# When a weight conversion's stages run beside attention: two orders of the same instructions

## The chip, the cores and the metric

The kernel runs on one core of a Trainium2 chip. The metric is the device time of one execution in microseconds (us); less is better. The engines named below: TensorE (PE; PEld is its loading of stationary operands), VectorE (DVE), ScalarE (ACT), GpSimd (POOL) and SyncE (SP, which here only issues DMAs). Each engine works through its own list of instructions in order; semaphores tie the lists together.

## The reference

An RWKV-6 attention is followed by a two-layer projection with a gated activation. All of it is float32 or wider.

```python
for t in range(S):                                   # B=4, H=8, S=768, D=48
    cur = np.einsum('bhd,bhe->bhde', u[None] * kt, vt)
    y[:, :, t] = np.einsum('bhd,bhde->bhe', rt, state + cur)
    state = wt[:, :, :, None] * state + np.einsum('bhd,bhe->bhde', kt, vt)
...
x = y.transpose(0, 2, 1, 3).reshape(B * S, H * D)    # 3072 tokens of 384
h = x @ w_in                                         # 384 x 2048
sp = np.maximum(h, 0.0) + np.log1p(np.exp(-np.abs(h)))
g = h * erf(sp)
out = g @ w_out                                      # 2048 x 384
```

The two weights come as 64-bit floats (the arrays are divided by a 64-bit square root), and the kernel itself turns them into float32.

## The kernel before

**Steps.** The work goes in 12 steps, counted from 0 here. A step is 128 tokens of a pair of batches. `attend(s, ...)` does the attention of steps 0 to 4, `attend_late` that of the later ones. The attention of a step runs over six levels: at level n, 32 pairs of small matmuls on TensorE (L444, in `level_products`) write products of k and r to a PSUM buffer, VectorE scales r and k by products of decays (L260, in `scale`), and VectorE copies the products under a mask into the tile `own` (L456; at level 1 it is a multiplication, L661; at level 6 ScalarE copies, L463). Level n+1 works on the scaled r and k. After level 6, `from_own` multiplies `own` by v on TensorE (L478), k is transposed (L673) and copied to `kT` by ScalarE (L677), `state_part` makes the state's increments (L530), and VectorE and GpSimd bring the state up to date (L703 or L701, L704, L706). `through_state` adds the old state's part (L504), and ScalarE copies y to `xT` (L511 to L514), part of it by six small DMAs (L518).

**PSUM buffers.** `products` hands out one of two buffers, `pp0` and `pp1`. While weights are being converted it always gives `pp0`, because the conversion uses `pp1`. Two further buffers, `m`, hold the results of the projections.

**The projections beside it.** Pieces of the feed-forward part are put between the levels, so that TensorE has work while VectorE and ScalarE finish a level: `hidden` makes two F tiles of h (L742, 12 matmul records a piece, then a copy to SBUF by ScalarE, L751), `project` multiplies the gated h by w_out (L771, result copied at L780). Softplus and erf (L724, L727, ScalarE) and the gating product (L731, VectorE) are taken from a list by `advance`. Steps 1 and 2 have only `hidden` pieces of the step before.

**The conversion.** The weights are turned from 64-bit to 32-bit floats in 16 pieces, 8 of w_in and 8 of w_out, in `convert`, a generator to which single letters are sent. One piece takes: a load by SyncE (`l`, L196) into one of three buffers `words`; a pair of ScalarE operations (`s`: L209 to `pp1` from the high words, L211 to `rest` from the low words); a shift in place by VectorE (`h`, L217, in `pp1`); an OR of the sign by VectorE (`o`, L225, which reads `words` and `pp1` and writes the weight); and an integer add of `rest` by GpSimd (L229). `j` stands for `ho`. The next `s` needs the `o` before it, for `pp1`; the load three pieces later needs that `o` too.

**The order.** Nothing is scheduled by a planner: the order in which the Python code issues instructions is the order on each engine. `place(n)` is called at the end of level n+1 (0 to 5), and then at 6 after the transposes and 7 after the state; it sends the letters of `CONVERT[s][n]`, then issues a projection piece. The letters for place 8 are sent by `behind()` at the step's end. In step 1 at level 2, `behind(None)` sends the letters of `BEHIND_SCALING` between the scaling and the masked copy. In step 1, `products(..., 1)` puts the state part into `pp1`.

```python
CONVERT = (
    ("", "", "", "", "", "s", "jls", "j", "sl"),
    ("hl", "jsl", "jsl", "jsl", "jl", "sj", "", "", "sl"),
    ("jsl", "jsl", "jsl", "jsl", "jl", "sj", "s"),
    ("js", "j"),
)
BEHIND_SCALING = "os"
```

## Time and profile before

| what | us |
|---|---|
| median of 3 runs (616.69, 619.03, 617.15) | 617.15 |
| the profiled execution | 616.69 |
| its span, first to last instruction | 614.9 |
| TensorE busy in the span | 602.1 |
| VectorE, ScalarE, GpSimd busy | 409.3, 293.9, 293.3 |
| L742 (first projection), TensorE busy, and L771 (second) | 257.3 and 252.1 |
| one piece of `hidden` on TensorE (L742 x12) | 2.86 |
| step 1 between the starts of its first and last L742 | 34.55 to 66.37 |
| step 2 likewise | 68.93 to 96.75 |

The profile page gives shares of the span by engine. The timeline that is quoted further down has one row for each instruction or run of equal ones: start in us from the span's start, length in us, engine, line, operation, output and inputs, and in square brackets the idle time of the engine before it, with what ended it. [...] "SPq" and "ACTq" rows are DMAs being issued. Matmul ends are modelled.

### The profile page before, as it was taken

The page shows a single profiled execution, that of the slowest core. Times are in us where ns is not written, and L with a number is a line of the kernel's source. Part 1 is how long each engine was busy: PE and PEld are TensorE (multiplying, and loading weights), DVE is VectorE, ACT ScalarE, POOL GpSimd, SP SyncE. Part 2 cuts the span into 40 slices and gives each one's busy share as a digit, 9 for nine tenths or more (in the row PEclk, how much of TensorE's full clock was granted, in tenths as well). Part 3 has the DMA queues.
Part 4 walks back from the last instruction along what each step waited for, and adds up shares of the span by engine and source line. Part 5 has one row for each costly group of instructions (what it writes and reads, how often), then busy time and mean ns, then how long its engine had stood idle before and what let it go on. Part 6 is the DMA issues. An engine that isn't in the chain of part 4 may idle for free.

```text
span 614.9 us, 15592 instructions
## 1 busy us (share of the span) xinstructions
PE 602.1 (98%) x6858; PEld 445.9 (73%) x6858; DVE 409.3 (67%) x459; ACT 293.9 (48%) x374; POOL 293.3 (48%) x295
## 2 busy tenths in 40 slices
PE   7889999999999999999999999999999999999997
PEld 6668787678668668668668768768768768668654
DVE  5687696995995897897797797797797311110300
ACT  2548888544446724534534534534534444624600
POOL 4348184603497399299199299299296000000000
PEclk9999999999999999999999999999999999999999
DMA  8376471440353316307307306405303100000000
GB/s 325 117 281 203 184 258 58 164 149 8 136 157 78 101 34 190 112 29 206 101 30 197 109 31 181 126 31 156 117 28 79 25 26 0 9 26 1 0 27 26
DMA packets 51371, 63.27 MB, mean 103 GB/s; under 512 B 34920, under 2 KB 40296, under 8 KB 49896
## 3 DMA queue, kind: packets, MB, share of 16 engines
q1 hardware_dynamic: 50152, 61.68, 31.5%
q8 instruction: 54, 0.88, 0.6%
q10 hardware_dynamic: 1152, 0.59, 0.4%
q14 instruction: 13, 0.11, 0.1%
HBM read 52.39 MB, written 8.69 MB: 99 GB/s over the span
## 4 chain that ended last, share of the span: by engine, by line
PE 85%; DVE 6%; DMA 3%; POOL 2%; issue 2%; ACT 1%; SPq 0%; POOLq 0%; ACTq 0%; DVEq 0%
PE m L771 38%; PE m L742 37%; PE pp L444 4%; DMA w<-in_rkw 3%; PE y L478 2%; PE y L504 1%; PE pp L530 1%; DVE in L260 1%; POOL w_in_sb L229 1%; DVE w_in_sb L225 1%; POOL tot_sb L312 1%; PE pp L673 1%; DVE sums L364 1%; DVE pp L217 1%; DVE own L456 1%
## 5 line engine op out<-in xcount | busy, mean ns | idle before, releaser
L742 PE MATMUL m<-xT,w_in_sb 128*128 128x256 f32 x1152 | 257.3, 382 | 2.4 <-DVE w_in_sb L225 1.2
L771 PE MATMUL m<-w_out_sb,h 128*128 128x384 f32 x768 | 252.1, 488 | 0.0
L742 PEld LDWEIGHTS m<-xT,w_in_sb 128*128 128x128 f32 x1152 | 216.1, 190 | 34.8 <-issue 3.6
L771 PEld LDWEIGHTS m<-w_out_sb,h 128*128 128x128 f32 x768 | 144.6, 190 | 98.5
L751 ACT COPY h<-m 128x512 f32<-128x512 f32 x96 | 56.1, 584 | 130.5 <-PE m L742 130.4
L731 DVE TENSOR_TENSOR h<-h,sp 128x1024 f32<-128x1024 f32 x48 | 74.6, 1594 | 52.1 <-ACT sp L727 51.9
L260 DVE TENSOR_TENSOR in<-in,tot_sb 128x1024 f32<-128x1024 f32 (+1 forms) x60 | 84.4, 1414 | 30.6 <-PE pp L444 27.3
L378 POOL TENSOR_TENSOR words<-words,rest 128x528 f32<-128x528 f32 (+10 forms) x77 | 85.7, 1113 | 6.0
L374 POOL TENSOR_TENSOR rk<-words 128x528 f32<-128x528 f32 (+3 forms) x28 | 44.5, 1588 | 81.2 <-DVE sums L364 70.8
L780 ACT COPY o<-m 128x384 f32<-128x384 f32 x24 | 11.5, 480 | 110.3 <-PE m L771 110.3
L312 POOL TENSOR_TENSOR tot_sb<-tot_sb 128x256 f32<-128x256 f32 (+4 forms) x60 | 54.6, 911 | 4.5
L727 ACT ACTIVATE sp<-sp 128x2048 f32<-128x2048 f32 x24 | 45.9, 1911 | 0.3
L724 ACT ACTIVATE sp<-h 128x2048 f32<-128x2048 f32 x24 | 45.9, 1911 | 0.3
L444 PEld LDWEIGHTS pp<-in 48*64 48x64 f32 (+1 forms) x2368 | 33.8, 125 | 16.3 <-issue 8.5
L364 DVE TENSOR_REDUCE sums<-words 128x6 f32<-128x288 f32 (+8 forms) x66 | 29.2, 470 | 19.4 <-POOL words L374 19.2
L444 PE MATMUL pp<-in 48*64 48x64 f32 (+1 forms) x2368 | 38.3, 212 | 3.7 <-issue 1.6
L727 ACT ACT_TABLE_LOAD x24 | 30.8, 1283 | 15.9 <-issue 13.0
L374 POOL TENSOR_TENSOR words<-words 128x336 f32<-128x336 f32 (+6 forms) x49 | 35.1, 716 | 3.8
L364 DVE TENSOR_REDUCE sums<-rk 128x14 f32<-128x672 f32 (+9 forms) x54 | 34.8, 704 | 0.2
L724 ACT ACT_TABLE_LOAD x24 | 30.8, 1283 | 4.9 <-issue 4.5
L378 DVE TENSOR_TENSOR words<-words,rest 128x576 f32<-128x576 f32 (+8 forms) x34 | 27.9, 820 | 1.2
L229 POOL TENSOR_TENSOR w_out_sb<-w_out_sb,rest 128x768 int32<-128x768 int32 x8 | 17.8, 2222 | 17.8 <-DVE w_out_sb L225 17.7
(80 smaller groups left out, 438.0 us busy)
## 6 DMA issues: line engine op xcount, KB each, us to landing
in<-in_rkw SPq DMA_DIRECT2D x11, 1024.0 KB, 5.6
words<-in_moe_w_in SPq DMA_DIRECT2D x8, 768.0 KB, 4.5
words<-in_moe_w_out SPq DMA_DIRECT2D x8, 768.0 KB, 4.3
words<-in_rk_rows SPq DMA_DIRECT2D x8, 768.0 KB, 6.8
w<-in_rkw SPq DMA_DIRECT2D x11, 512.0 KB, 8.4
v<-in_v SPq DMA_DIRECT2D x12, 384.0 KB, 6.9
out<-o SPq DMA_DIRECT2D x24, 192.0 KB, 1.9
rest<-in_w_rows SPq DMA_DIRECT2D x8, 384.0 KB, 7.3
```

Of the source, the lines that this page charges most:

```text
L260: nc.vector.tensor_mul(halves, halves, view(tots[level - 1], 0, [[1, n], [2, nb], [0, half]]))
L312: nc.gpsimd.tensor_mul(new, pair[:, :, 0], pair[:, :, 1])
L364: nc.vector.tensor_reduce(out=view(sums[:], n, [[near * (NEAR + 1), NEAR // near], [NEAR + 1, near - n]]), in_=terms[n], axis=mybir.AxisLi ...
L374: engine.tensor_mul(terms[n], r[:, :, n:], k[:, :, : near - n])
L378: engine.tensor_mul(k[:, :, :m], k[:, :, :m], w[:, :, n : n + m])
L444: nc.tensor.matmul(pp[s0 : s0 + m, e, n, :m], lhsT=rk[rows(e), 1, n, s0 : s0 + m], rhs=rk[rows(e), 0, n, t0 : t0 + m], start=True, stop=True,)
L724: nc.scalar.activation(held[0][:], h[:], AF.Softplus)
L727: nc.scalar.activation(held[0][:], held[0][:], AF.Erf)
L731: nc.vector.tensor_mul(h[:, part], h[:, part], held[0][:, part])
L742: nc.tensor.matmul(ps[:, ff, :], lhsT=w_in_sb[:, g * FG + f + ff, kk * P : (kk + 1) * P], rhs=xT[:, kk, :], start=kk == 0, stop=kk == KT - 1,)
L751: nc.scalar.copy(h[:, f : f + FT, :], ps[:])
L771: nc.tensor.matmul(ps[j][:], lhsT=gs[g][:, f, j * C : (j + 1) * C], rhs=w_out_sb[:, g * FG + f, :], start=g + f == 0, stop=g == NG - 1 and ...
```

## The change

The stages of the conversion take other places in steps 1 and 2, and the state part of step 1 takes the other PSUM buffer. No instruction is added or taken away on any engine:

- VectorE: in step 1 at level 2, the OR (L225) comes before the scaling (L260), not after it.
- ScalarE: in step 1, one pair L209, L211 (piece 3) comes ahead of the first copy L751 of the step. In steps 1 and 2 at level 6, one pair (pieces 7 and 13) comes ahead of the second of two copies L751 and of the copies of `own` (L463), not after them. In step 2 the pair after that (piece 14) comes behind L463, ahead of the copies of h and `kT`, not after `kT`.
- TensorE: the order is the same; the state part of step 1 (L530) writes `pp0`, and so the first products of step 2 (L444) get a wait for VectorE (L706).
- GpSimd and SyncE: the same order.

```diff
--- before.py
+++ after.py
@@ -125,11 +125,9 @@
 
     turns = {"next": 0, "converting": False}
 
-    def products(shape, n=None):
-
-
-        if n is not None:
-            return ps_p.tile(shape, FP32, name=f"pp{n}")
+    def products(shape):
+
+
         n = 0 if turns["converting"] else turns["next"]
         turns["next"] = 1 - n
         return ps_p.tile(shape, FP32, name=f"pp{n}")
@@ -211,35 +209,29 @@
                 nc.scalar.mul(out=rest[:], in_=low.bitcast(U32), mul=2.0**-29)
                 held[i] += [base.bitcast(I32), rest]
 
-        def shift(i):
-            if i in held:
-                bits = held[i][1]
-                nc.vector.tensor_scalar(
-                    out=bits, in0=bits, scalar1=3, scalar2=None, op0=ALU.logical_shift_left
-                )
-
         def join(i):
             if i in held:
                 words, bits, rest = held.pop(i)
                 into = weights[i][0].bitcast(I32)
+                nc.vector.tensor_scalar(
+                    out=bits, in0=bits, scalar1=3, scalar2=None, op0=ALU.logical_shift_left
+                )
                 nc.vector.scalar_tensor_tensor(
                     out=into, in0=words[:, :, :, 1], scalar=-(1 << 31), in1=bits,
                     op0=ALU.bitwise_and, op1=ALU.bitwise_or,
                 )
                 nc.gpsimd.tensor_tensor(out=into, in0=into, in1=rest[:], op=ALU.add)
 
-        stages = {"l": load, "s": scale, "h": shift, "o": join}
-        done = dict.fromkeys(stages, 0)
+        done = {"l": 0, "s": 0, "j": 0}
         for _ in range(3):
             load(done["l"])
             done["l"] += 1
         while True:
             what = yield
-            for stage in {"j": "ho"}.get(what, what):
-                stages[stage](done[stage])
-                done[stage] += 1
+            {"l": load, "s": scale, "j": join}[what](done[what])
+            done[what] += 1
             if weights[0][1].dtype != FP32:
-                turns["converting"] = 0 < done["s"] and done["o"] < len(weights)
+                turns["converting"] = 0 < done["s"] and done["j"] < len(weights)
                 turns["next"] = 0
 
     def rows(e, n=D):
@@ -652,8 +644,6 @@
             keep_busy(DM, DM // 2)
             if level == 1 and s == 1:
                 stay_warm()
-            if s == 1 and level == 2:
-                behind(None)
             got = pp[:].rearrange("p e n t -> p (e n) t")
             if level == 1:
                 if not s:
@@ -687,8 +677,7 @@
 
 
         if s:
-
-            ps = products([P, NC, JP, HC], 1 if s == 1 else None)
+            ps = products([P, NC, JP, HC])
             ps = [ps[:, h] for h in range(NC)]
         else:
             ps = [ps_m.tile([P, JP, HC], FP32, name="m") for h in range(NC)]
@@ -827,12 +816,10 @@
 
     CONVERT = (
         ("", "", "", "", "", "s", "jls", "j", "sl"),
-        ("hl", "jsl", "jsl", "jsl", "jl", "sj", "", "", "sl"),
-        ("jsl", "jsl", "jsl", "jsl", "jl", "sj", "s"),
+        ("jsl", "jsl", "jsl", "jsl", "jsl", "j", "", "", "sl"),
+        ("jsl", "jsl", "jsl", "jsl", "jsl", "js"),
         ("js", "j"),
     )
-
-    BEHIND_SCALING = "os"
 
     STAGES = {
         1: (0, 0, 0, 0, 0, 0, 1, 0), 2: (1, 0, 0, 0, 0, 0, 1, 1), 3: (1, 2, 1, 0, 0, 2, 1, 1)
@@ -900,14 +887,7 @@
             if s > DIRECT:
                 attend_late(s, place)
                 continue
-            def behind(n=0):
-                if n is not None:
-                    convert_at(LOG + 2)
-                    return
-                for what in BEHIND_SCALING:
-                    conversion.send(what)
-
-            attend(s, xTs[s], place, behind)
+            attend(s, xTs[s], place, lambda: convert_at(LOG + 2))
             if s + 2 < n_steps:
                 load_step(s + 2)
                 if s + 2 == DIRECT:
```

## The prediction

> **What bounds the kernel now.** I read the page from the top: busy shares, then the chain that ended last, then the same chain in order of time, and last the timeline of steps 1 and 2 (counted from 0; the change's words call them steps two and three), where every moved instruction stands.

> From the page, busy times and the shares of the chain:

> ```profile
> PE 602.1 (98%) x6858; PEld 445.9 (73%) x6858; DVE 409.3 (67%) x459; ACT 293.9 (48%) x374; POOL 293.3 (48%) x295
> ...
> PE 85%; DVE 6%; DMA 3%; POOL 2%; issue 2%; ACT 1%; SPq 0%; POOLq 0%; ACTq 0%; DVEq 0%
> ```

> TensorE bounds nearly everything. So the change is worth what it adds to or takes from TensorE's waits between 35 and 105 us; no instruction is added or removed on any engine. Where TensorE has a wait, some other engine is the bound for a moment. The first one is at level 2 of step 1 (timeline: start, length, engine, line):

> ```profile
> 39.02 1.23 DVE L260 TENSOR_TENSOR in<-in,tot_sb 128x1024 f32<-128x1024 f32 x1 [1.41 <-PE pp L444]
> 40.16 0.95 DVE L225 SCALAR_TENSOR_TENSOR w_in_sb<-words,pp 128x768 int32<-128x768 int32 x1
> 41.03 1.34 DVE L456 COPY_PREDICATED own<-mask_sb,pp 128x512 f32<-128x512 int32 x1
> 41.14 0.88 ACT L209 ACTIVATE pp<-words 128x768 f32<-128x768 f32 x1 [2.66 <-DVE w_in_sb L225]
> 41.17 7.06 SPq L196 DMA_DIRECT2D words<-in_moe_w_in  x3
> 41.25 1.83 POOL L229 TENSOR_TENSOR w_in_sb<-w_in_sb,rest 128x768 int32<-128x768 int32 x1 [3.96 <-DVE w_in_sb L225]
> ...
> 42.52 1.16 PE L444 MATMUL pp<-in 48*64 48x64 f32 x64 [0.78 <-DVE own L456]
> ```

> VectorE idles 1.41 us for the level's products, then runs the scaling, the OR of a weight piece and the masked copy; TensorE waits 0.78 us for that copy. Two other places show what VectorE's scaling costs when a GpSimd add (L229) is already running:

> ```profile
> 71.80 1.83 POOL L229 TENSOR_TENSOR w_out_sb<-w_out_sb,rest 128x768 int32<-128x768 int32 x1 [6.71 <-DVE w_out_sb L225]
> ...
> 73.23 1.49 DVE L260 TENSOR_TENSOR in<-in,tot_sb 128x1024 f32<-128x1024 f32 x1 [1.57 <-PE pp L444]
> ...
> 117.56 2.41 POOL L229 TENSOR_TENSOR w_out_sb<-w_out_sb,rest 128x768 int32<-128x768 int32 x1
> 118.34 2.25 DVE L378 TENSOR_TENSOR words<-words,rest 128x576 f32<-128x576 f32 x1
> ```

> The scaling takes 1.49 instead of 1.22 us when it meets the last 0.40 us of the add, and ends 1.09 us after it. The second pair is the strong case: a product of 576 elements takes 2.25 us where its neighbour of 672 took 0.86, and it ends 0.62 us after the add.

> The ends of the two steps, level 6 and what follows:

> ```profile
> 54.26 0.59 ACT L751 COPY h<-m 128x512 f32<-128x512 f32 x1 [0.29 <-PE m L742]
> 54.27 0.95 DVE L225 SCALAR_TENSOR_TENSOR w_in_sb<-words,pp 128x768 int32<-128x768 int32 x1
> 54.95 1.18 ACT L463 COPY own<-pp 32x512 f32<-32x512 f32 x2
> 55.04 2.86 PE L742 MATMUL m<-xT,w_in_sb 128*128 128x256 f32 x12
> 56.04 0.86 ACT L209 ACTIVATE pp<-words 128x768 f32<-128x768 f32 x1
> 57.83 0.67 PE L478 MATMUL y<-own,v 64*48 64x64 f32 x32
> ...
> 65.13 1.12 DVE L706 TENSOR_TENSOR s<-faded,pp 48x384 f32<-48x384 f32 x2 [0.95 <-POOL faded L704]
> 65.33 1.11 PE L444 MATMUL pp<-rk 48*64 48x64 f32 x64
> ...
> 68.93 3.14 PE L742 MATMUL m<-xT,w_in_sb 128*128 128x256 f32 x12 [1.00 <-DMA xT<-y]
> ...
> 87.88 0.95 DVE L225 SCALAR_TENSOR_TENSOR w_out_sb<-words,pp 128x768 int32<-128x768 int32 x1
> 88.55 1.18 ACT L463 COPY own<-pp 32x512 f32<-32x512 f32 x2
> 89.64 0.86 ACT L209 ACTIVATE pp<-words 128x768 f32<-128x768 f32 x1
> 91.23 0.67 PE L478 MATMUL y<-own,v 64*48 64x64 f32 x32
> ```

> In both steps the copies of own (L463) end well before TensorE's L478 needs them, because ScalarE does its next conversion pair (L209, L211) after them. The chain in order of time shows that step 1 ends on ScalarE, not TensorE: from kT at 59.55 without a gap through the softplus, y, xT and its DMA to 68.93.

> **The change part by part.** Weight pieces are numbered from 0; #2 is the first one joined in step 1.

> *1. Level 2 of step 1: the OR moves ahead of the scaling.* VectorE's order becomes shift, OR, scaling, copy. The shift starts at 36.66 and an OR follows a shift by 1.0 us (26.52 to 27.53), so the OR runs 37.66 to 38.61, in what was idle. Taken alone this ends the scaling at 40.25 and the copy at 41.5, and TensorE's level 3 would start when L742 ends, 41.74: a gain of 0.78. But the OR releases GpSimd's add, which follows its end by 0.14 (41.11 to 41.25): 38.75 to 40.58. The scaling comes at 39.02, behind it. By the 71.80 row it ends 1.09 after the add, at 41.67, instead of 40.25. The copy starts 0.09 before that end (as at 40.16) and takes 1.34: 42.92. TensorE follows by 0.15: 43.06, against 42.52. **Loss 0.54.** [...]
> Bounds: -0.78 (no meeting) to +0.67 (its whole 1.22 run after the add); I take 0.54, by the nearest row. In before the scaling starts first and the add waits (2.68 us at 44.36); at levels 3 to 5 both queues move by the same 0.54, so that order stays.
> Moved with it: ScalarE's pair #3 goes ahead of the copy of h (37.90 to about 40.35); the buffer it frees is wanted by the L742 of 43.61, so the 3 us between hide it. The load that waits for the OR (SP, 41.17) goes out at 38.65; its piece is first used at 47.87+0.54, and the slowest later landing was 9.2 us, so it is in time. What it shares the queues with, step 2's inputs, is wanted from 49.97.

> *2. Level 6 of step 1: pair #7 goes ahead of the second copy of h and of L463.* L209 must wait for the OR of #6 to free its PSUM buffer. In the clock of before: OR ends 55.22, L209 at 55.26, L211 0.84 later, the copy of h 0.82 later (56.92), L463 0.49 later, 57.41 to 58.59. TensorE would start L478 at 57.90. Its first two matmuls need only the first half of own; the third starts at 58.65, and the remaining 14 of 16 take 0.52: 59.17 against 58.49. **Loss 0.68** (bounds: 0.1, if the first half's end at 58.0 were enough, to 1.0 with 0.15 of latency at each of two hand-overs). Behind L478 stand the transposes, kT and the whole ScalarE chain to 68.93: it moves by 0.54+0.68.

> *3. Step 1's state part in the first buffer.* L444 of the next step must now wait for L706, ending at 66.25: it starts at 66.35 instead of 65.33, 1.02 late. Behind it: its own 1.04 and six matmuls (66.37 to 67.93, 1.56), then the L742 that waits until 68.93 for xT. That wait of 1.00 takes it: 66.35+1.04+1.56 = 68.95. **Loss 0.0 to 0.1, 0.05 taken.** If xT came earlier, up to 1.0 would show.

> *4. Level 6 of step 2: pair #13 likewise.* OR ends 88.83; L209 88.87, L211 89.71, copy of h 90.53, L463 91.02 to 92.20. L478 starts its third matmul at 92.25 and ends 92.77, against 91.30+0.59 = 91.89. **Loss 0.88** (bounds 0.3 to 1.2, worked like part 2). Here TensorE has no other wait: every row from 72.07 to 145.77 in the chain is its own, so all of it counts. Pair #14 now precedes the copies of h and kT: kT ends at 95.05 instead of 93.75, and the state part that needs it starts at 95.44+0.88; hidden by one L742 group of 2.75.

> *Downstream.* At 146.77 VectorE starts on TensorE's L530 after an idle 5.80, and carries the chain to 171.74; it starts later by what TensorE is late. Nothing there is tied to a fixed time, so I subtract nothing.

> *Sum.* 0.54+0.68+0.05+0.88 = 2.15 us. The profiled execution took 616.69 (span 614.9 and 1.8 around it): 618.84. It is 0.46 below the median of 617.15, so against the median: 619.3.

> **The rivals.**
> *A, the add does not block the scaling.* Then part 1 gains 0.78, part 2 gives 0.68 back, part 3's tie holds step 1's end where it is, and only part 4 counts: 617.15+0.88 = 618.0. For it: at 9.38 the scaling beside short GpSimd products took only 1.53. Against: the 118.34 row.
> *B, not slower.* One place, 146 to 172: VectorE's chain there takes up the delay because ScalarE's and GpSimd's results, not TensorE's, set its pace; price -2.15, time 617.2. It decides if the work at 146.77 could start 2 us later and the level at 171.74 were still on time. For it: there is 1.42 and 0.80 of issue time inside this stretch of the chain. Against: the 5.80 wait at its head and the 0.33 that TensorE waits at its end.
> [...]
> A fall of the granted clock I count under C: the rows show 1.00 throughout, even in 32 to 36 us, where TensorE was busy 2.75 of 4; the new waits (1.3, 0.8, 1.0, 0.9) leave no longer gap. [...]

> **How the numbers follow.** Sum as worked out: 0.5. A: 0.17. B: 0.08. C: 0.25. The likeliest is 619.3. Their bounds give 617.9 (0.3 for part 1, 0.1, 0, 0.3) to 620.1 (0.67, 1.0, 0.1, 1.2); to hold 8 in 10 I reach to A below and C above: 617.6 to 620.9. The 0.5% that a measurement can tell from no change is 3.1 us: slower means over 620.24, most of C and a tail of the sum, since the three runs of before lie 2.3 apart: 0.27. Faster (under 614.06) has no case of its own: 0.02. The rest, 0.71, lies within.

> **What the profile after would show.** Part 1: the OR near 37.7, the add near 38.75, the scaling longer than 2 us, the level-3 L444 near 43.1. Part 2 and 4: L209 before L463, and L478 waiting 0.7 to 1.0 on ScalarE's own. Part 3: the rk L444 waiting about 1 us on L706 and the wait on xT gone or nearly. Wrong if the scaling keeps 1.23, if L478 does not wait, if the granted clock falls, or if the delay at 100 us differs from the delay at 175 us.

## The result, and the profile after

The changed kernel took 620.38 us (median of 4 runs, 620.20 to 620.52) where the kernel before took 617.30 on the same chip (4 runs, 616.69 to 619.03): a ratio of 1.0045 with a 95% interval of 1.0025 to 1.0066. That is 3.1 us or 0.5% more. The profiled execution took 620.44 us, with a span of 618.7; against the profiled execution before (616.69) it is 3.75 longer. 620.38 lies inside the range forecast, 1.1 above the value forecast. As will be seen, the sum of the four parts was priced well (2.15, measured 2.06), and 1.8 us of the 3.75 came from a place that was priced at nothing.

In the changed kernel the lines named here are numbered 2 to 11 lower: L444 has become L436, L260 L252, L225 L219, L229 L223, L456 L448, L209 L207, L463 L455, L478 L470, L706 L695, L742 L731, L504 L496, L771 L760.

The page of the changed kernel, busy times and the shares of the chain that ended last:

```profile
PE 602.6 (97%) x6858; PEld 446.0 (72%) x6858; DVE 411.5 (67%) x459; ACT 293.4 (47%) x374; POOL 292.8 (47%) x295
...
PE 86%; DVE 7%; issue 2%; ACT 2%; DMA 1%; POOL 1%; SPq 0%; DVEq 0%; ACTq 0%; POOLq 0%
```

TensorE works as long as before (602.6 against 602.1), so the added time is TensorE standing still. Level 2 of step 1, in the timeline of the changed kernel (start, length, engine, line, and in brackets the idle time and what ended it):

```profile
37.55 0.95 DVE L219 SCALAR_TENSOR_TENSOR w_in_sb<-words,pp 128x768 int32<-128x768 int32 x1
38.64 1.83 POOL L223 TENSOR_TENSOR w_in_sb<-w_in_sb,rest 128x768 int32<-128x768 int32 x1 [1.46 <-DVE w_in_sb L219]
38.92 2.64 DVE L252 TENSOR_TENSOR in<-in,tot_sb 128x1024 f32<-128x1024 f32 x1 [0.42 <-PE pp L436]
41.48 1.27 DVE L448 COPY_PREDICATED own<-mask_sb,pp 128x512 f32<-128x512 int32 x1
42.90 1.16 PE L436 MATMUL pp<-in 48*64 48x64 f32 x64 [1.26 <-DVE own L448]
```

GpSimd's add starts 0.28 ahead of VectorE's scaling, which then takes 2.64 in place of 1.23 and ends 1.09 after the add (41.56 against 40.47). TensorE waits 1.26 in place of 0.78. The ends of steps 1 and 2 and the start of step 2, in the same view:

```profile
55.65 0.88 ACT L207 ACTIVATE pp<-words 128x768 f32<-128x768 f32 x1 [1.29 <-DVE w_in_sb L219]
57.73 1.17 ACT L455 COPY own<-pp 32x512 f32<-32x512 f32 x2
58.95 0.65 PE L470 MATMUL y<-own,v 64*48 64x64 f32 x28 [0.28 <-ACT own L455]
...
66.25 1.11 DVE L695 TENSOR_TENSOR s<-faded,pp 48x384 f32<-48x384 f32 x2 [0.95 <-POOL faded L693]
67.51 1.16 PE L436 MATMUL pp<-rk 48*64 48x64 f32 x64 [0.88 <-DVE s L695]
68.60 1.78 PE L731 MATMUL m<-xT,w_in_sb 128*128 128x256 f32 x7
...
90.04 0.88 ACT L207 ACTIVATE pp<-words 128x768 f32<-128x768 f32 x1 [1.30 <-DVE w_out_sb L219]
92.11 1.17 ACT L455 COPY own<-pp 32x512 f32<-32x512 f32 x2
93.33 0.65 PE L470 MATMUL y<-own,v 64*48 64x64 f32 x28 [0.28 <-ACT own L455]
```

At both step ends ScalarE does the conversion pair first, the copies of own come late, and all but four of the matmul records that read own follow the second copy. At 67.51 TensorE waits 0.88 for VectorE, and the 1.00 that it waited before on xT is gone: L731 goes straight on at 68.60.

Following one marker after another through both traces (start in the changed kernel less start before, us):

| marker | delay |
|---|---|
| step 1's first shift (chance difference of the start) | -0.11 |
| level 3 of step 1 | +0.38 |
| transposes after level 6, step 1 | +1.12 |
| level 2 of step 2 | +1.17 |
| transposes after level 6, step 2 | +2.09 |
| first L771 (101.73 before) | +1.94 |
| the L771 after VectorE's stretch (172.74 before) | +1.95 |
| L504 run at 249.31 before | +1.97 |
| what follows that run | +2.17 |
| L504 run at 435.62 before | +2.19 |
| what follows that run | +3.75 |
| last run of L771 (570.21 before) | +3.75 |

The last jump is the surprise. It lies 330 us behind the last changed instruction, where both kernels issue the same instructions. The chain in order of time (start, length, what), first of the kernel before, then of the changed one:

```profile
435.62 1.19 PE y L504 x64
436.81 5.36 PE m L771 x16
```

```profile
437.81 0.33 PE y L496 x21
438.14 1.55 issue
439.69 0.87 PE y L496 x43
440.56 1.49 PE m L760 x4
```

In the middle of a run of 64 small matmul records, with nothing to wait for, TensorE issues nothing for 1.55 us ("issue" is time in which the engine waited for nothing that the profile shows). The same run takes 2.75 in place of 1.19. A gap of the same kind near 250 us exists in both kernels (0.94 before, 1.09 after); the run around it took 2.05 before and 2.24 after, which is the other +0.20.

### The profile page after: what moved, and what is told of

It reads as the page before. It is cut to its first block, busy times and chain, and to the rows that moved or that the text cites. A ratio compares the mean times of both kernels' runs of the same rounds, so it can differ in the third digit from the quotient of the medians.

```text
span 618.7 us, 15586 instructions
## 1 busy us (share of the span) xinstructions
PE 602.6 (97%) x6858; PEld 446.0 (72%) x6858; DVE 411.5 (67%) x459; ACT 293.4 (47%) x374; POOL 292.8 (47%) x295
## 4 chain that ended last, share of the span: by engine, by line
PE 86%; DVE 7%; issue 2%; ACT 2%; DMA 1%; POOL 1%; SPq 0%; DVEq 0%; ACTq 0%; POOLq 0%
PE m L760 38%; PE m L731 37%; PE pp L436 5%; DVE in L252 2%; PE y L470 2%; PE pp L522 1%; PE y L496 1%; DMA in<-in_rkw 1%; PE pp L663 1%; DVE pp L216 1%; DVE sums L356 1%; DVE words L370 1%; DVE own L448 1%; DVE w_in_sb L219 0%; ACT own L455 0%
## 5 line engine op out<-in xcount | busy, mean ns | idle before, releaser
L731 PE MATMUL m<-xT,w_in_sb 128*128 128x256 f32 x1152 | 257.2, 382 | 1.4 <-DVE w_in_sb L219 1.2
L760 PE MATMUL m<-w_out_sb,h 128*128 128x384 f32 x768 | 252.1, 488 | 0.0
L731 PEld LDWEIGHTS m<-xT,w_in_sb 128*128 128x128 f32 x1152 | 216.1, 190 | 33.7 <-issue 2.4
L760 PEld LDWEIGHTS m<-w_out_sb,h 128*128 128x128 f32 x768 | 144.6, 190 | 98.5
L252 DVE TENSOR_TENSOR in<-in,tot_sb 128x1024 f32<-128x1024 f32 (+1 forms) x60 | 85.9, 1440 | 29.9 <-PE pp L436 28.2
L304 POOL TENSOR_TENSOR tot_sb<-tot_sb 128x256 f32<-128x256 f32 (+4 forms) x60 | 52.8, 880 | 4.5
L436 PEld LDWEIGHTS pp<-in 48*64 48x64 f32 (+1 forms) x2368 | 33.8, 125 | 16.6 <-issue 10.5
L436 PE MATMUL pp<-in 48*64 48x64 f32 (+1 forms) x2368 | 38.4, 212 | 4.1 <-DVE own L448 1.4
L223 POOL TENSOR_TENSOR w_out_sb<-w_out_sb,rest 128x768 int32<-128x768 int32 x8 | 17.8, 2231 | 18.3 <-DVE w_out_sb L219 18.3
```

The source lines that it names most:

```text
L252: nc.vector.tensor_mul(halves, halves, view(tots[level - 1], 0, [[1, n], [2, nb], [0, half]]))
L304: nc.gpsimd.tensor_mul(new, pair[:, :, 0], pair[:, :, 1])
L436: nc.tensor.matmul(pp[s0 : s0 + m, e, n, :m], lhsT=rk[rows(e), 1, n, s0 : s0 + m], rhs=rk[rows(e), 0, n, t0 : t0 + m], start=True, stop=True,)
L731: nc.tensor.matmul(ps[:, ff, :], lhsT=w_in_sb[:, g * FG + f + ff, kk * P : (kk + 1) * P], rhs=xT[:, kk, :], start=kk == 0, stop=kk == KT - 1,)
L760: nc.tensor.matmul(ps[j][:], lhsT=gs[g][:, f, j * C : (j + 1) * C], rhs=w_out_sb[:, g * FG + f, :], start=g + f == 0, stop=g == NG - 1 and ...
```

## The experiments

### One part at a time

Each of the four parts was made alone; what was expected stands under each edit.

Part 1:

```diff
-            if s == 1 and level == 2:
-                behind(None)
...
-        ("hl", "jsl", "jsl", "jsl", "jl", "sj", "", "", "sl"),
+        ("jsl", "jsl", "jsl", "jsl", "jl", "sj", "", "", "sl"),
```

> The kernel before with part 1 alone: in step 1 at level 2 the OR of weight piece 2 precedes the scaling, and with it pair 3 precedes the first copy of h. [...]

Part 2:

```diff
-        ("hl", "jsl", "jsl", "jsl", "jl", "sj", "", "", "sl"),
+        ("hl", "jsl", "jsl", "jsl", "jsl", "j", "", "", "sl"),
```

> The kernel before with part 2 alone: in step 1 at level 6, pair 7 precedes the second copy of h and the copies of own. Theory (one chain OR, L209, L211, copy of h, copy of own, products): the products from own wait 0.6 to 0.8 us on ScalarE, kT and the DMA of xT move by the same, the time rises by 0.7 us. Rival (ScalarE catches up before xT, or the 1.0 us wait for xT takes it): the time is the same within 0.2 us.

Part 4:

```diff
-        ("jsl", "jsl", "jsl", "jsl", "jl", "sj", "s"),
+        ("jsl", "jsl", "jsl", "jsl", "jsl", "js"),
```

> The kernel before with part 4 alone: in step 2 at level 6, pair 13 precedes the second copy of h and the copies of own, and pair 14 precedes the copy of kT. Theory: the products from own wait 0.9 us on ScalarE, and nothing behind takes it up: the time rises by 0.9 us. Rival (something behind it takes it up, or adds to it): the delay at the start of step 3 and that at the end of the span differ.

Part 3:

```diff
-            ps = products([P, NC, JP, HC], 1 if s == 1 else None)
+            ps = products([P, NC, JP, HC])
```

> The kernel before with part 3 alone: the state part of step 1 goes to the first PSUM buffer. Theory: the first products of step 2 wait about 1.0 us for the state update, the wait for xT that follows them vanishes, and the time changes by 0.0 to 0.1 us. Rival (the wait adds to that for xT): the time rises by 1.0 us. If the four parts are all that the change does, the four differences sum to 2.0 to 2.2 us; what the change measured beyond that (3.1 in all) must then come from waits of TensorE that belong to no part, as those near 252 and 438 us of the changed kernel's profile.

Measured, against 617.37 for the kernel before on that chip (35 runs). The delay is that of the L771 at 172.74, less the delay of step 1's first shift. Such differences repeat to about 0.1 us: the two kernels with one matmul more, further down, give 0.08 where part 3 alone gives 0.15, and 2.12 where the whole change gives 2.06.

| part | median | ratio, 95% interval | delay at 172.74 | forecast |
|---|---|---|---|---|
| 1 | 617.26 | 1.0002 [0.9993, 1.0011] | 0.59-0.08 = 0.51 | 0.54 |
| 2 | 617.86 | 1.0014 [0.9998, 1.0030] | 0.58+0.15 = 0.73 | 0.68 |
| 4 | 617.71 | 1.0008 [0.9997, 1.0019] | 0.98-0.14 = 0.84 | 0.88 |
| 3 | 619.31 | 1.0030 [1.0017, 1.0043] | 0.17-0.02 = 0.15 | 0.05 |
| sum | | | 2.23 | 2.15 |
| all four (against 617.30) | 620.38 | 1.0045 [1.0025, 1.0066] | 1.95+0.11 = 2.06 | 2.15 |

The traces show parts 1, 2 and 4 at the sizes forecast. The times alone do not: these parts are 0.1% each, and the intervals of all three hold 1.

In part 1 alone, the scaling again runs long (VectorE's and TensorE's rows):

```profile
39.11 2.63 DVE L260 TENSOR_TENSOR in<-in,tot_sb 128x1024 f32<-128x1024 f32 x1 [0.42 <-PE pp L444]
...
43.10 1.16 PE L444 MATMUL pp<-in 48*64 48x64 f32 x64 [1.27 <-DVE own L456]
```

So rival A is false. In parts 2 and 4 alone, TensorE's records that read `own` follow ScalarE's second copy, all but four, as in the changed kernel (one row from each run):

```profile
58.43 0.65 PE L478 MATMUL y<-own,v 64*48 64x64 f32 x28 [0.28 <-ACT own L463]
...
92.36 0.65 PE L478 MATMUL y<-own,v 64*48 64x64 f32 x28 [0.28 <-ACT own L463]
```

And part 3, which delays steps 1 and 2 by next to nothing, is the dearest by the clock, 1.9 us. Its trace has the gap that the changed kernel has, and a long one near 250 us (chain in order of time):

```profile
250.21 1.63 issue
251.84 0.44 PE y L504 x15
252.28 4.15 PE m L771 x7
```

and near 437 us:

```profile
438.21 0.32 PE y L504 x21
438.53 1.50 issue
440.04 0.87 PE y L504 x43
```

### What part 3 does to TensorE's list

Part 3 moves no instruction. But in the built program TensorE's list is shorter by three: of the instructions that do nothing but wait for a semaphore, it has 91 where the kernel before has 94. Parts 1, 2 and 4 leave that list as it was. So "No instruction is added or taken away on any engine" holds for the work alone: with the change TensorE, ScalarE and VectorE lose three, two and one separate waits, and the profile pages count 15592 instructions before and 15586 after. Counting an entry for each separate wait and four for each small matmul (two weight loads and two matmuls, as in the trace), the gaps can be placed in the list. In the kernel before the gap near 250 us stands behind 48 of the 64 records, in lists three shorter behind 49; counted from the start both are entry 7698, within one. The gap near 437 us is at 11538, in every kernel in which it shows. The two are 15 x 256 entries apart. The kernel before also has gaps in step 0, 0.95 us at entry 450 and 0.62 at entry 706: 256 apart. Its rows (TensorE in the timeline, then the chain):

```profile
15.64 0.56 PE L444 MATMUL pp<-in 48*64 48x64 f32 x18 [0.95 <-issue]
21.56 0.68 PE L444 MATMUL pp<-in 48*64 48x64 f32 x26 [0.62 <-issue]
...
249.31 0.67 PE y L504 x48
249.98 0.94 issue
```

The two pairs are not on one grid of 256 by this count: from 706 to 7698 are 27 x 256 entries and 80 more. A gap at entry 2002, which two kernels further down have (the repeated product and the shorter list), is 5 x 256 and 16 behind 706. Why is not known.

Two explanations were left for the gap near 437: that the kernel is late there (another engine or a DMA then meets it), or that the following work has moved in the list. To make the kernel late with TensorE's list as it was, a VectorE product of 1.6 us is done twice on the chain of step 4:

```diff
-        nc.vector.tensor_mul(
+        for _ in range(2 if s == DIRECT else 1):
+            nc.vector.tensor_mul(
...
```

> The kernel before with one VectorE product of about 1.5 us done twice (the by_tokens product that opens own of step 4, near 151 us); TensorE's list is not touched. It asks whether the 1.5 us gap of TensorE near 438 us comes from everything being later, or from TensorE's list having three wait instructions fewer. If from the list: the gap near 436 stays at or under 0.3 us, and the time rises by the 1.3 to 1.7 us of the product alone. If from lateness: the gap appears here too, and the time rises by 2.8 to 3.2 us.

The two products took 2.98 us, the one before 1.63, and the run in question, now at 439.96, took 0.95 with no gap (L504 is L505 there; the row counts 62 of the 64 records):

```profile
439.96 0.95 PE y L505 x62
```

Lateness does not make it. The median was 619.30 against 617.01 (ratio 1.0033 [1.0023, 1.0043]), 0.9 more than the product; the profiled execution (620.80) also lost 1.3 us in step 0, where four records of a dummy matmul took 2.29 in place of 1.24, and 1.33 in a gap at 52.7, neither of them at the edit. Whether the same makes the excess of the median is open.

Then the list was moved back. One small matmul of step 2's level 2 is done twice (four entries), first with part 3 alone, so that the list is one entry longer than before, then with the whole change:

```diff
+            if (s, level) == (2, 2):
+                nc.tensor.matmul(
+                    pp[:HC, 0, 0, :HC], lhsT=rk[rows(0), 1, 0, :HC],
+                    rhs=rk[rows(0), 0, 0, :HC], start=True, stop=True,
+                )
```

> The state part of step 1 in the first buffer (as the run with that part alone, 619.3 us), and one small matmul of step 2 level 2 done twice, which puts four instructions into TensorE's list for the three waits that went. Theory (the position of TensorE's instructions in its list sets the gaps): the gap near 438 falls to 0.3 us or less and the time to 617.4 to 617.8. Rival (the wait for the state update costs the time itself): the time stays at 619.3.

> The changed kernel with the same doubled small matmul. Position theory: the gap near 438 goes, the time falls by about 1.3 us to 618.8 to 619.3, where the four parts' sum of 2.0 puts it. Rival: it stays at 620.4.

Part 3 with one more matmul took 617.17 against 617.01 (ratio 0.9998 [0.9988, 1.0008]): the 1.9 us are gone. Its chain at the same place:

```profile
435.76 0.32 PE y L504 x19
436.08 0.14 issue
436.22 0.88 PE y L504 x45
```

The whole change with one more matmul took 619.06 (5 runs; ratio 1.0031 [1.0019, 1.0043]), and the run of 64 records took 1.07:

```profile
439.47 1.07 PE y L496 x64
```

So without the late gap the change costs 2.05 us by the medians, where 2.15 was forecast; the late gap is then about 1.0 of the 3.1.

Last, the reverse: the kernel before, without part 3, with its list four entries shorter or longer. In the shorter one TensorE leaves out a dummy matmul of step 0 that only keeps it busy; in the longer one it does the small matmul above twice.

```diff
-            keep_busy(DM, DM // 2)
+            keep_busy(DM, *(() if level == 3 else (DM // 2,)))
```

> Before, with one of the two dummy matmuls that TensorE does at level 3 of step 0 left out (0.43 of the 1.24 us of that group; it keeps TensorE busy in a wait and feeds nothing). TensorE's list is then 4 entries shorter; no buffer, no wait and no other engine's order is changed. Theory of the list's position: the gap late in the kernel comes from where the following instructions lie in the list, so it must appear here too, without the other buffer: a gap of 1.0 to 1.6 us in the L504 run near 436 us (before: a row of 1.19 in place of 0.90, 0.29), and a median of 618.3 to 619.3. Rival, the buffer itself: no gap above 0.3 there, median 616.8 to 617.5.

> Before, with one small matmul of step 2's level 2 done twice: TensorE's list is 4 entries longer and nothing else changes. Theory of the list's position: 1 entry more gave a gap of 0.14 at 436 us, none more 0.29; 4 more should give none or one below 0.3, and a median of 616.8 to 617.4 (the matmul itself takes 0.02). Rival, any change of the list disturbs the supply: a gap of 1 us or more somewhere behind 250 us that before does not have, median above 618.

The shorter one has the gap, without the buffer:

```profile
440.66 0.33 PE y L504 x22
440.99 1.75 issue
442.74 0.87 PE y L504 x42
```

Its median is 619.61 against 617.16 (ratio 1.0036 [1.0017, 1.0055]). Not all of that is the gap: in the profiled execution (625.22) TensorE's granted clock fell to 0.50 from 19 to 27 us, soon after the place (16.4) where the dummy was missing. The longer one took 616.68 (0.9993 [0.9984, 1.0002]) and its run 0.90 us, the shortest of all:

```profile
435.61 0.90 PE y L504 x64
```

Put together, the run of 64 records near 437 us by the length of TensorE's list. The last column is explained below.

| entries against before | kernels | length of the run, us | instruction transfer begins ahead of the run, us |
|---|---|---|---|
| -4 | the shorter list | 2.95 | 0.3 |
| -3 | the whole change; part 3 alone | 2.75; 2.69 | 0.8; 0.8 |
| 0 | before; parts 1, 2, 4 alone; the repeated product | 1.19; 1.16, 1.34, 0.95; 0.95 | 2.2; 2.3, 2.0, 2.2; 2.3 |
| 0 | the add held at one place, at two (next section) | 1.23; 1.16 | 2.2; 2.3 |
| +1 | part 3 and one matmul; the change and one matmul | 1.34; 1.07 | 2.3; 2.4 |
| +4 | the longer list | 0.90 | 2.6 |

The place of the list at which the gap stands is fixed, and a list shorter by three or four makes it 1.5 us or more, with the buffer changed or not. The traces point to instructions as what TensorE lacks there. The profile has a queue of instruction transfers, 54 of them with 0.88 MB in both kernels: 16.3 KB each, and 54 x 256, the distance inside the first pair of gaps, is 13,824 where TensorE's list has 13,895 entries. That a transfer brings about 256 entries of this list is an estimate from these counts. Each of the 41 gaps without a wait that are over 0.2 us, in all 13 traces, ends 2.3 to 2.9 us after one of these transfers began and 1.2 to 1.6 us after it ended. Near 437 us that transfer begins at 433.44 in the kernel before, 437.05 in the changed one and 440.32 in the shorter list (the last column of the table sets it against the start of the run): the later it begins, the longer the gap. The distances inside the two pairs, 256 and 15 x 256, agree with the estimate. At these places, in runs of small matmuls, TensorE stood for 0 to 1.75 us. Why three or four entries less let the transfer begin 1.4 to 1.8 us later against the run than in the kernel before was not settled.

### Holding the add back

If the add that runs beside the scaling is what part 1 loses by, then the OR may go first as long as the add does not. In this version the OR precedes the scaling, and the add of that piece waits on GpSimd behind a copy of one element of the scaled tile (lines are 9 or 10 higher in this kernel):

```diff
+                nc.gpsimd.tensor_copy(out=after_scaling[:], in_=loaded[s][0][:, 0, 0, 2:3])
+                turns["add"]()
...
-        ("hl", "jsl", "jsl", "jsl", "jl", "sj", "", "", "sl"),
+        ("hosl", "jsl", "jsl", "jsl", "jl", "sj", "", "", "sl"),
```

> The kernel before with the OR of piece 2 ahead of the scaling as in part 1, but GpSimd's add of that piece is held until the scaling is done, by a one-element GpSimd copy that reads what the scaling wrote. [...] Rival (the scaling is long for another reason, the OR's place or the pair on ScalarE): the scaling still takes about 2.6 us and the time does not fall.

```profile
39.16 1.23 DVE L270 TENSOR_TENSOR in<-in,tot_sb 128x1024 f32<-128x1024 f32 x1 [0.51 <-PE pp L454]
40.45 0.19 POOL L666 COPY after_scaling<-in 128x1 f32<-128x1 f32 x1 [3.12 <-DVE in L270]
40.59 1.81 POOL L238 TENSOR_TENSOR w_in_sb<-w_in_sb,rest 128x768 int32<-128x768 int32 x1
41.81 1.16 PE L454 MATMUL pp<-in 48*64 48x64 f32 x64
```

The scaling is back at 1.23, TensorE's level 3 starts at 41.81 where it was 42.52 in the kernel before, and the time is 616.28 against 617.01 (ratio 0.9988 [0.9979, 0.9996]). With the same at level 2 of step 2 (`HELD = {1, 2}`):

> The version with the GpSimd add held behind the scaling at level 2 of step 1, with the same done at level 2 of step 2. There the scaling took 1.49 us instead of 1.23 and TensorE's level 3 waited 0.17 for what followed. [...]

It took 616.03 against 617.16 (ratio 0.9978 [0.9966, 0.9991]): faster than both kernels. Step 2's scaling took 1.23 in place of 1.49, and TensorE's wait of 0.17 there is gone:

```profile
72.55 1.23 DVE L270 TENSOR_TENSOR in<-in,tot_sb 128x1024 f32<-128x1024 f32 x1 [1.58 <-PE pp L454]
```

Between the one place and the two the times cannot tell.

## Why the prediction was right, and where not

- **Part 1, 0.54.** Right in mechanism and size: 0.51 alone, 0.49 in the changed kernel. The scaling ended 1.09 after the add, as the row at 71.80 gave it; a full run of the scaling after the add, which the upper bound (0.67) stood for, would have ended 0.14 later (1.23). That the add is the cause is shown by holding it back: the scaling takes 1.23 again, and this brings the gain of 0.7 that the lower bound (-0.78) stood for. By what means the add holds up the scaling, no run shows.
- **Part 2, 0.68.** 0.73 alone, 0.74 in the changed kernel. L470 starts its later matmuls at 58.95, behind ScalarE's second copy, and only four records (two matmuls) go ahead, as worked out.
- **Part 3, 0.05, as a wait.** At its place right: TensorE waits 0.88 on L695 and the wait for xT takes it up; 0.05 is left in the changed kernel, 0.15 alone. As a whole it is the part that failed, because of the next point.
- **Part 4, 0.88.** 0.84 alone, 0.92 in the changed kernel.
- **Downstream, "Nothing there is tied to a fixed time, so I subtract nothing".** Nothing was subtracted and nothing was added, and this is the term that was wrong: +1.78 in the profiled execution (0.20 at 250 us, 1.56 at 437, 0.02 between them). What is tied there is not a time but a place in TensorE's list, entry 11538, where TensorE stood 1.55 us and went on 2.64 us after a transfer of instructions had begun (437.05 to 439.69). Part 3 was read as "the order is the same"; the list's length was not looked at, and it is three waits shorter.
- **The sum.** 2.15 forecast; 2.06 by the trace at 172.74, 2.05 by the time of the changed kernel with its list moved back. The time itself rose by 3.1, because of the late gap. That 620.38 still lies in the range is luck: the bounds of the parts end at 620.1, and the reach above that was kept for C.
- **The rivals.** A fell with the 2.64 of the scaling. B fell with +1.94 before VectorE's stretch and +1.95 behind it: its chain passes on the whole delay. The 0.25 of C and the reach up to 620.9 stood for a long scaling at level 5 of step 1. No run shows it: in the changed kernel that scaling, at 51.89, took 1.24, and the granted clock stayed at 1.00. A time above the value forecast was reached by another way, the gap near 437.

## What to carry to other kernels

Before an OR, a copy or any release is moved ahead, look at what it sets free on GpSimd: here the scaling, starting 0.28 behind the add, took 2.64 in place of 1.23 and ended 1.09 after it, and holding the add behind the scaling by a cheap dependence (a copy of 0.19) brought the scaling back to 1.23 and kept the gain of 0.7. When a change that moves no work costs time far away from it, compare the gaps inside runs of small matmuls and count where they stand in TensorE's list; adding one small matmul is a quick test, and the start of the instruction transfer ahead of the gap shows whether it came late (0.8 ahead of the run in the changed kernel, 2.2 in the kernel before). And take a sum of part effects from markers in the traces, since times of 0.1% cannot carry them.

## What the runs showed of the hardware

The longest gaps cost a second time. After the 1.50 and the 1.55 the next 64 L771 records took 20.84 us, after the 1.63 and the 1.75 they took 22.53. The windows of the shorter list after the 1.75 (the stretch, its length, busy times of the five engines, then the granted clock, the DMA share and GB/s):

```profile
440.40:443.50 3.10, 1.35 (x84) 1.16 (x73) 3.10 (x4) 0.00 (x0) 0.00 (x0) 1.00 0.00 0
443.50:445.50 2.00, 2.00 (x9) 1.12 (x5) 1.93 (x3) 1.20 (x4) 0.00 (x0) 0.70 0.04 8
445.50:447.50 2.00, 2.00 (x5) 1.06 (x4) 1.90 (x4) 0.81 (x1) 0.00 (x0) 0.50 0.19 48
447.50:449.50 2.00, 2.00 (x7) 1.23 (x6) 1.93 (x3) 1.99 (x2) 0.00 (x0) 0.94 0.86 268
```

The granted clock goes to 0.50 for a while and the run loses 1.69 us, which at half clock is 3.4 us of it, an estimate. TensorE was idle for 1.75 of the 3.10 us ahead of the fall. What sets the clock down was not shown, and the gap alone does not decide: in step 0 dummy matmuls slowed to 2.29 behind a gap of 1.21 in the kernel with the repeated product, and kept their 1.24 behind a gap of 1.33 in part 4 alone.
